# Turning a bias with DVE and ACT instead of TensorE, in the prologue of a fused LayerNorm-MLP kernel

## The chip, the cores and the metric

The kernel runs on one core of one Trainium2 chip. The metric is device time in microseconds, as the median of several executions; lower is better. A profile of one execution lies beside it, and times inside the text are counted from the start of that execution's span.

## The reference

```python
B, S, D, F = 1, 2048, 1024, 3584      # bfloat16 x, w1, b1, w2, b2

def reference(x, w1, b1, w2, b2):
    y = _layernorm(x, axis=-1)        # no scale, no shift, eps 1e-5
    h = _gelu(jnp.einsum("bsd,df->bsf", y, w1) + b1)     # tanh form
    return jnp.einsum("bsf,fd->bsd", h, w2) + b2
```

The bias `b1` has 3584 values. The kernel computes the hidden layer transposed, with the hidden index on the partitions, so `b1` must stand as 28 columns of 128 partitions (`b1_sb`, float32). There ACT takes one column as the per-partition bias of each Gelu.

## The kernel before

Rows of x are handled in 16 tiles of 128 rows, four tiles to a block of 512. The hidden dimension is cut into 28 row blocks of 128 (`FT = 28`), the model dimension into 8 blocks of 128 (`DT = 8`). For each block of x the first product makes `hT_sb` (28 row blocks, 8 matmuls of 128x128x512 each, line 370), ACT applies bias and Gelu out of PSUM (line 396), and the second product goes through all 28 row blocks for each output tile (line 438), after which DVE adds `b2` (line 449) and SP stores. While TensorE works on one block, DVE normalises and transposes the next (lines 254 to 310).

The first block is different, because nothing is there yet. It goes as follows.

- SP issues the loads of x tiles and w1 pieces in a fixed order. ACT's queue issues two loads: `b1`, then the first w1 piece (`w0`). Tile 0 of x is the first load on SP's queue.
- TensorE runs 25 warm-up matmuls on constants (line 460). Then, in the order of the program, it turns `b1` (`pe_b1`, line 521), transposes x tiles 0 and 1 against an identity (line 331), and begins a "wave" of eight row blocks (`pe_wave`, line 386) on the raw, not yet centred tiles 0 to 2, with the transposes of half of tile 2 in between. Tile 3 enters the wave last, normalised.
- ACT copies the transposed tiles out of PSUM (line 343), casts the turned bias into `b1_sb` (`put_b1`, line 525), moves part of tile 2 (`put_moves_2`, line 509), spreads the row of means over the partitions (`put_row_spread`, line 475), moves part of tile 3 (line 516), and only then begins the Gelus.
- DVE takes the statistics of tiles 0 to 3 (lines 254, 264), turns the other half of tile 2 by 32x32 blocks (`turn_2`, line 492), turns means and reciprocal deviations into rows (line 469), normalises tile 3 and turns it (lines 268, 479), centres the raw tiles (line 538), and corrects the raw products in PSUM (`ops_fix`, lines 545 and 548).
- POOL computes the reciprocal deviations (line 261) and moves the remaining blocks of tiles 2 and 3 (lines 505, 484).

Each engine works through its own list strictly in order. The lists are written out by `pe.op`, `act.op`, `dve.op`, `pool.op` and `sp.op`, each with the events that it waits for and the event that it signals; `_emit` turns them into semaphore waits. The list of DVE for the first block is the sequence `seq`. Names of events that the text uses: `b1` (load landed), `b1t` (bias turned), `b1c` (bias in `b1_sb`; every Gelu waits for it), `xq2` (half of tile 2 turned by DVE), `tup2` and `tua2` (moved by POOL and by ACT), `te3`, `tg3`, `tc3` (tile 3 moved), `row_0` and `row_1` (rows spread).

The bias goes through three steps. It is loaded as 28 rows of 128 values into `b1r_sb`. TensorE turns it against a 28x28 corner of the identity into PSUM bank 1 of `ps_1`, and ACT casts the 128x28 result into `b1_sb`. The event of that cast is also recorded as the last reader of the bank, so the wave's second unit waits for it.

Of the kernel before, what the change touches and what calls it, by code (L numbers as in the profile page):

```python
# [7 lines left out]
BF16 = mybir.dt.bfloat16  # L8
F32 = mybir.dt.float32
# [3 lines left out]
P = 128  # L13
# [83 lines left out]
def bass_standalone__mixer_channel_mlp__prompt_kernel(  # L97
# [11 lines left out]
    F = w1.shape[1]  # L109
    NT = ST // P  # L110
    DT = D // P
    FT = F // P
# [2 lines left out]
    DH = D // NCH  # L115
    HC = D // 2
    assert ST % TB == 0 and D % P == 0 and F % P == 0 and D % NCH == 0
    assert HC <= 512 and DT * P * 2 <= 2048 and FT >= 4 and FT <= P
    R = R_WAVE
    assert R == NB1 + NB2 + 1 and R < FT  # L120
    assert NB1 + NB2 + 1 <= 8 and NB2 == 2
# [25 lines left out]
    with ExitStack() as es:  # L147
        sb = lambda name, shape, dt: es.enter_context(nc.sbuf_tensor(name, shape, dt))
# [6 lines left out]
        hT_sb = sb("hT_sb", [P, FT, TB], BF16)  # L155
        o_sb = sb("o_sb", [P, NOB, D], BF16)
        b2_sb = sb("b2_sb", [P, D], BF16)
        b1r_sb = sb("b1r_sb", [FT, P], BF16)
        b1_sb = sb("b1_sb", [P, FT], F32)
        ident = sb("ident", [P, P], BF16)  # L160
        ones = nc.const_aps.tensor(1.0, [P, P], BF16)
        stat_r = sb("stat_r", [P, len(RAW), 4], F32)
# [17 lines left out]
        pe = _Prog("s_pe")  # L180
        act = _Prog("s_act")
# [10 lines left out]
        def dma(dst, src, sig, nbytes, waits=()):  # L192
            dma_q[0].op(lambda e, dst=dst, src=src: e.dma_start(dst, src), waits=waits, sig=sig, sem="d_" + sig, inc=16)
            dma_bytes[0] += nbytes
            est[sig] = DMA_T0 + dma_bytes[0] / DMA_BYTES_PER_US

        def load_x_tile(i):
            dma(x_sb[:, i, :], xf[i * P:(i + 1) * P, :], f"x{i}", P * D * 2)
            x_ev[i] = (f"x{i}", f"x{i}")
# [7 lines left out]
        def load_w1(ci):  # L207
            j0, j1, a, b = w1_chunks[ci]
            dma(w1_sb[:, j0:j1, a:b], w1v[:, j0:j1, a:b], f"w1c{ci}", (j1 - j0) * P * (b - a) * 2)
            w1_issued.add(ci)  # L210
# [5 lines left out]
        def issue(item):  # L216
            if item == "b1":
                dma_q[0] = act
                dma(b1r_sb[:, :], b1.rearrange("(t p) -> t p", p=P), "b1", F * 2)
                dma_q[0] = sp  # L220
            elif item[0] == "x":
                load_x_tile(int(item[1:]))
            elif item[0] == "w" and int(item[1:]) < len(w1_chunks):
                dma_q[0] = act if item == "w0" else sp
                load_w1(int(item[1:]))
                dma_q[0] = sp

        act.op(lambda e: e.preload_act_table(ACT.Gelu_apprx_tanh))
        for item in SP_FIRST_LOADS:
            issue(item)  # L230
# [8 lines left out]
        for b in range(2, NB):  # L239
# [4 lines left out]
                sig="ident")  # L244
# [7 lines left out]
        def op_stats(i, h):  # L252
            pw = D // parts(i)
            return (lambda e, i=i, h=h, pw=pw: e.bn_stats(st_sb[i][:, 6 * h:6 * (h + 1)],  # L254
                                                          x_sb[:, i, h * pw:(h + 1) * pw]),
                    [x_ev[i][h if len(x_ev[i]) == parts(i) else 0]], f"st{i}_{h}", 0.03 + pw * 0.0012)

        def op_aggr(i):
            mv = stat_r[:, i, 0:2] if i in RAW else mv_sb[:, i, :]
            dst = stat_r[:, i, 2:3] if i in RAW else rstd_sb[:, i:i + 1]  # L260
            pool.op(lambda e, i=i, dst=dst, mv=mv: e.tensor_tensor(out=dst, in0=mv[:, 1:2], in1=nhalf[:, i:i + 1],  # L261
                                                                   op=ALU.pow),
                    waits=[f"mv{i}", "nhalf"] + (["tup2"] if i == 1 else []), sig=f"rstd{i}")
            return (lambda e, i=i, mv=mv: e.bn_aggr(mv, st_sb[i][:, :]),  # L264
                    [f"st{i}_{parts(i) - 1}", f"eps{i}"], f"mv{i}", 0.33)
# [9 lines left out]
        def ops_norm(i):  # L275
            cuts = (0, DT)
            y_ev[i] = []
            res = []
            for k, (j0, j1) in enumerate(zip(cuts[:-1], cuts[1:])):
                res.append(op_norm(i, j0 * P, j1 * P, f"y{i}_{k}"))  # L280
                y_ev[i] += [f"y{i}_{k}"] * (j1 - j0)
            return res
# [32 lines left out]
        def dve_put(o):  # L315
# [3 lines left out]
        bank_read = {}  # L319
        bank_of = {"t": ps_t[:, 0, :], "2_0": ps_2b[:, 0, :], "2_1": ps_2b[:, 1, :], "1_1": ps_1b[:, 1, :], "1_2": ps_1b[:, 2, :], "1_3": ps_1b[:, 3, :],  # L320
                   "1_4": ps_1b[:, 4, :]}
# [40 lines left out]
        def unit_bank(bank):  # L362
            return ps_tf if bank[0] == "t" else (ps_1 if bank[0] == "1" else ps_2)[:, bank[1], :]
# [30 lines left out]
        def act_gelu(r, t0, t1, bank, wait_ev, sig):  # L394
            n0, n1 = t0 * P, t1 * P
            act.op(lambda e, r=r, n0=n0, n1=n1, bank=bank: e.activation(  # L396
                out=hT_sb[:, r, n0:n1], in_=unit_bank(bank)[:, n0:n1], func=ACT.Gelu_apprx_tanh,
                bias=b1_sb[:, r:r + 1], scale=1.0),
                waits=[wait_ev, "b1c"], sig=sig)
            bank_gelu[bank] = sig  # L400

# [76 lines left out]
        def moves_3():  # L478
            res = [(lambda e: e.transpose(out=xq_sb[:, :], in_=x_sb[:, 3, :]), [y_ev[3][-1], "tua2", "tup2"], "xq", 1.07)]
            for tq, q in POOL_MOVES + DVE_MOVES:  # L480
                src = xq_sb[32 * tq:32 * (tq + 1), :].rearrange("p (j q s) -> p j q s", j=DT, q=4)[:, :, q, :].bitcast(I32)
                dst = yT_sb[32 * q:32 * (q + 1), ybuf(0), :, ycol(3) + 32 * tq:ycol(3) + 32 * (tq + 1)].bitcast(I32)
                if (tq, q) in POOL_MOVES:
                    pool.op(lambda e, src=src, dst=dst: e.tensor_copy(out=dst, in_=src), waits=["xq"],
                            sig=("tg3" if (tq, q) == POOL_MOVES[-1] else None))
                if (tq, q) in DVE_MOVES:
                    res.append((lambda e, src=src, dst=dst: e.tensor_copy(out=dst, in_=src), ["xq"],
                                ("tc3" if len(res) == len(DVE_MOVES) else None), 0.2))
            return res

        def turn_2():
            return [(lambda e: e.transpose(out=xq_sb[:, 0:(DT - N_TURN) * P], in_=x_sb[:, 2, N_TURN * P:]),
                     [x_ev[2][0]], "xq2", 0.64)]

        def put_moves_2(eng):
            todo = POOL_TURNS
            if eng is act:
                todo = [m for m in ((tq, q) for tq in range(4) for q in range(4)) if m not in POOL_TURNS]
            for n, (tq, q) in enumerate(todo):
                src = xq_sb[32 * tq:32 * (tq + 1), 0:(DT - N_TURN) * P]  # L500
                src = src.rearrange("p (j q s) -> p j q s", j=DT - N_TURN, q=4)[:, :, q, :].bitcast(I32)
                dst = yT_sb[32 * q:32 * (q + 1), 0, N_TURN:DT, ycol(2) + 32 * tq:ycol(2) + 32 * (tq + 1)].bitcast(I32)
                sig = "tup2" if eng is pool else "tua2"
                if eng is pool:
                    pool.op(lambda e, src=src, dst=dst: e.tensor_copy(out=dst, in_=src),
                            waits=["xq2"] + {0: ["rstd0"], 4: ["tup2_0"]}.get(n, []),
                            sig={3: "tup2_0", 7: sig}.get(n))
                else:
                    act.op(lambda e, src=src, dst=dst: e.copy(out=dst, in_=src), waits=["xq2"], sig=(sig if n + 1 == len(todo) else None))
# [7 lines left out]
                       sig=("te3" if (tq, q) == todo[-1] else None))  # L517
            yT_ev[3] = ["te3"] * DT

        def pe_b1():  # L520
            pe.op(lambda e: e.transpose(out=bank_of["1_1"][:, 0:FT], in_=b1r_sb[:, :], identity=ident[0:FT, 0:FT]),  # L521
                  waits=["ident", "b1"], sig="b1t")

        def put_b1():
            act.op(lambda e: e.copy(out=b1_sb[:, :], in_=bank_of["1_1"][:, 0:FT]), waits=["b1t"], sig="b1c")
            bank_read["1_1"] = "b1c"

        row_b = lambda k: row_r[:, :, :].rearrange("p (t k) s -> p t k s", k=2)[:, :, k, :]
        raw_cols = lambda bank, c0: unit_bank(bank)[:, c0:c0 + len(RAW) * P].rearrange("p (t s) -> p t s", t=len(RAW))
# [21 lines left out]
        st = {0: [op_stats(0, 0), op_stats(0, 1), op_aggr(0)]}  # L551
        put_moves_2(pool)
        st.update({i: [op_stats(i, 0), op_stats(i, 1), op_aggr(i)] for i in range(1, TPB)})
        nm = {3: ops_norm(3)}
        turn_m, turn_r = ops_row_turn(0), ops_row_turn(1)
        ctr = ops_centre()
        seq = st[0] + st[1][:1] + turn_2() + st[1][1:] + st[2] + turn_m[:2] + st[3] + turn_m[2:] + nm[3] + moves_3() + turn_r + ctr[:2]
        for o in seq:
            dve_put(o)

        pe_b1()
        put_b1()
        T_BANKS = (("t", "2_0"), ("2_1", "1_4"), ("t", "2_0"))
        for t, j in [(0, j) for j in range(N_AHEAD)] + [(1, j) for j in range(GROUPS[1])] + [
                (0, j) for j in range(N_AHEAD, DT)] + [(1, j) for j in range(GROUPS[1], DT)]:
# [19 lines left out]
        for k in range(2):  # L585
            put_copy(2, G2, T_BANKS[2], k)
        put_moves_2(act)
        for j in range(N_TURN, DT):
            yT_ev[2][j] = "tua2"
        put_row_spread(0, 1, 4)  # L590
# [136 lines left out]
```

## Time and profile before

| | |
|---|---|
| median of 3 runs | 396.33 us (396.06 to 396.37) |
| profiled execution, its own time | 396.51 us |
| its span | 395.3 us |
| TensorE matmul busy | 390.9 us (99% of the span), 1916 instructions |
| DVE busy | 162.7 us (41%) |
| ACT busy | 87.1 us (22%) |
| POOL busy | 14.0 us (4%) |
| line 438 (second product) | 193.3 us of TensorE |
| line 370 (first product, blocks after the wave) | 152.4 and 31.9 us of TensorE |
| line 386 (the wave) | 14.4 and 3.2 us of TensorE |

A line of the time line gives the start of a group of instructions, its length, the engine, the source line, the operation, what it writes and reads, how many there are, and in brackets the idle time of the engine ahead of it and what ended that. "PEld" is the weight load of TensorE, which overlaps its matmuls ("PE"); "SPq" and "ACTq" are DMA issues on those engines' queues. Matmuls are pipelined, so that the length of one in the list is longer than the distance to the next.

### The profile page before, as it was taken

Reading aid. Unit: us, or ns where it says so; the run is one execution under the profiler, and the core shown is the slowest. Engines: PE = TensorE matmul, PEld = TensorE weight load, DVE = VectorE, ACT = ScalarE, POOL = GpSimd, SP = SyncE. Lnnn points to the kernel's source line nnn. Section 1 sums busy time; section 2 is a strip of 40 time slices with the busy share of each in tenths; the row PEclk is TensorE's granted clock in tenths of the full one; section 3 lists DMA queues with packets and bytes.
Section 4 is the critical chain, followed back from the end, with each engine's and each line's share of the span. In section 5 each row is a group of like instructions: output and inputs, shape, how many; then the busy total and the mean of one; then the engine's idle time right before and its main releaser. Section 6 shows DMA issues by size and latency. Waiting matters only on the chain.

```text
span 395.3 us, 4562 instructions
## 1 busy us (share of the span) xinstructions
PE 390.9 (99%) x1916; PEld 185.8 (47%) x1950; DVE 162.7 (41%) x339; ACT 87.1 (22%) x145; POOL 14.0 (4%) x69
## 2 busy tenths in 40 slices
PE   9999999999999999999999999999999999999998
PEld 8744444444444444444444444444444444444444
DVE  6998889998999306987100000001100000001011
ACT  5655420000134332000023443000003334400000
POOL 5201000011001100000000000000000000000000
PEclk9999999999999999999999999999999999999999
DMA  7999930000000000000000000000000000000000
GB/s 273 375 385 387 387 139 27 15 27 14 28 0 0 2 0 0 28 27 15 27 13 2 0 0 2 13 13 28 25 15 15 0 2 0 0 15 27 13 28 27
DMA packets 16078, 23.63 MB, mean 60 GB/s; under 512 B 1082, under 2 KB 8250, under 8 KB 16058
## 3 DMA queue, kind: packets, MB, share of 16 engines
q1 hardware_dynamic: 15872, 23.20, 16.5%
q8 instruction: 15, 0.25, 0.3%
q10 hardware_dynamic: 186, 0.14, 0.1%
q14 instruction: 5, 0.04, 0.0%
HBM read 19.14 MB, written 4.19 MB: 59 GB/s over the span
## 4 chain that ended last, share of the span: by engine, by line
PE 99%; issue 0%; DVE 0%
PE ps L438 49%; PE ps L370 38%; PE ps_t L370 7%; PE ps L386 3%; PE ps L460 1%; PE ps_t L386 0%; PE ps L331 0%; PE ps_t L331 0%; DVE o_sb L449 0%; PE ps L521 0%
## 5 line engine op out<-in xcount | busy, mean ns | idle before, releaser
L438 PE MATMUL ps<-w_sb,hT_sb 128*128 128x512 bf16 (+2 forms) x909 | 193.3, 373 | 0.8
L370 PE MATMUL ps<-yT_sb,w_sb 128*128 128x512 bf16 x678 | 152.4, 379 | 0.9
L438 PEld LDWEIGHTS ps<-w_sb,hT_sb 128*128 128x128 bf16 x924 | 88.6, 98 | 105.2
L396 ACT ACTIVATE hT_sb<-ps,b_sb 128x512 bf16<-128x512 f32 x94 | 64.0, 688 | 234.9 <-PE ps L370 217.2
L370 PEld LDWEIGHTS ps<-yT_sb,w_sb 128*128 128x128 bf16 x696 | 68.1, 98 | 81.9
L449 DVE TENSOR_TENSOR o_sb<-ps,b_sb 128x512 bf16<-128x512 f32 (+2 forms) x33 | 22.3, 676 | 198.7 <-PE ps L438 198.5
L310 DVE STREAM_TRANSPOSE yT_sb<-x_sb 32x256 bf16<-32x256 bf16 x192 | 83.7, 436 | 21.9 <-PE ps_t L370 18.8
L370 PE MATMUL ps_t<-yT_sb,w_sb 128*128 128x512 bf16 x135 | 31.9, 379 | 0.1
L254 DVE BATCH_NORM_STATS2 st_sb<-x_sb 128x6 f32<-128x512 bf16 x32 | 21.1, 671 | 3.5 <-DMA x_sb<-in_x_dram 3.4
L370 PEld LDWEIGHTS ps_t<-yT_sb,w_sb 128*128 128x128 bf16 x136 | 13.3, 98 | 16.1
L396 ACT ACTIVATE hT_sb<-ps_t,b_sb 128x512 bf16<-128x512 f32 x18 | 12.4, 687 | 17.1 <-PE ps_t L370 14.6
L386 PE MATMUL ps<-yT_sb,w_sb 128*128 128x128 bf16 (+3 forms) x132 | 14.4, 262 | 0.0
L386 PEld LDWEIGHTS ps<-yT_sb,w_sb 128*128 128x128 bf16 x132 | 10.0, 101 | 2.8
L261 POOL TENSOR_TENSOR rstd_sb<-mv_sb,nhalf 128x1 f32<-128x1 f32 x13 | 7.1, 548 | 111.7 <-DVE mv_sb L264 111.7
L412 DVE TENSOR_TENSOR ps<-ps,row_r 128x384 f32<-128x384 f32 x17 | 9.2, 563 | 3.1 <-PE ps L370 2.8
L268 DVE TENSOR_SCALAR x_sb<-x_sb,mv_sb,rstd_sb 128x1024 bf16<-128x1024 bf16 x13 | 7.0, 541 | 2.0 <-POOL rstd_sb L261 1.3
L545 DVE SCALAR_TENSOR_TENSOR ps<-row_r,ncs,ps 128x384 f32<-128x384 f32 x7 | 4.2, 614 | 0.5 <-PE ps L386 0.5
L548 DVE TENSOR_TENSOR ps<-ps,row_r 128x384 f32<-128x384 f32 x7 | 3.9, 563 | 0.2
L538 DVE TENSOR_TENSOR yT_sb<-yT_sb,row_r 128x768 bf16<-128x768 bf16 x4 | 3.6, 952 | 0.0
L460 PE MATMUL ps<-const-bfloat16-1.0 128*128 128x128 bf16 x25 | 2.8, 312 | 0.8 <-PEq L712 0.8
L475 ACT COPY row_r<-row_r 32x384 f32<-32x384 f32 x6 | 3.1, 509 | 2.2 <-DVE row_r L469 2.1
L386 PE MATMUL ps_t<-yT_sb,w_sb 128*128 128x386 bf16 (+1 forms) x16 | 3.2, 273 | 0.0
(37 smaller groups left out, 36.9 us busy)
## 6 DMA issues: line engine op xcount, KB each, us to landing
w_sb<-in_w_dram SPq DMA_DIRECT2D x4, 1792.0 KB, 18.3
w_sb<-in_w_dram SPq DMA_DIRECT2D x2, 2048.0 KB, 15.8
out_dram<-o_sb SPq DMA_DIRECT2D x31, 128.0 KB, 1.7
x_sb<-in_x_dram SPq DMA_DIRECT2D x3, 1024.0 KB, 14.5
w_sb<-in_w_dram SPq DMA_DIRECT2D x7, 256.0 KB, 5.5
x_sb<-in_x_dram SPq DMA_DIRECT2D x4, 256.0 KB, 3.3
w_sb<-in_w_dram SPq DMA_DIRECT2D x1, 1024.0 KB, 9.3
b_sb<-in_b_dram SPq DMA_DIRECT2D x1, 256.0 KB, 14.4
```

What stands on the lines that cost most here:

```text
L254: return (lambda e, i=i, h=h, pw=pw: e.bn_stats(st_sb[i][:, 6 * h:6 * (h + 1)], x_sb[:, i, h * pw:(h + 1) * pw]), [x_ev[i][h if len(x_ev[i ...
L261: pool.op(lambda e, i=i, dst=dst, mv=mv: e.tensor_tensor(out=dst, in0=mv[:, 1:2], in1=nhalf[:, i:i + 1], op=ALU.pow), waits=[f"mv{i}", "nh ...
L268: return (lambda e, i=i, c0=c0, c1=c1: e.tensor_scalar(out=x_sb[:, i, c0:c1], in0=x_sb[:, i, c0:c1], scalar1=mv_sb[:, i, 0:1], scalar2=rst ...
L310: res.append((lambda e, src=src, dst=dst: e.transpose(out=dst, in_=src), waits, (f"tr{i}" if lastop else None), 0.47))
L370: pe.op(lambda e, b=b, r=r, dt=dt, bank=bank: e.matmul(unit_bank(bank)[:, 0:TB], lhsT=w1_sb[:, dt, r * P:(r + 1) * P], rhs=yT_sb[:, ybuf(b ...
L386: pe.op(lambda e: e.matmul(unit_bank(bank)[:, n0:n1], lhsT=w1_sb[:, dt, r * P:(r + 1) * P], rhs=yT_sb[:, 0 if tiles[0] in RAW else ybuf(0) ...
L396: act.op(lambda e, r=r, n0=n0, n1=n1, bank=bank: e.activation(out=hT_sb[:, r, n0:n1], in_=unit_bank(bank)[:, n0:n1], func=ACT.Gelu_apprx_tanh,
L412: crit.append((est[sig], (lambda e, reg=reg: e.tensor_tensor(out=reg, in0=reg, in1=row_b(1), op=ALU.mult), [sig, "row_1"], ready, 0.57), 0))
L438: pe.op(lambda e, sl=sl, ft=ft, c0=c0, c1=c1, bank=bank: e.matmul(ps_2[:, bank, 0:c1 - c0], lhsT=hT_sb[:, ft, sl * P:(sl + 1) * P], rhs=w2 ...
L449: crit.append((est[sig], (lambda e, ob=ob, c0=c0, c1=c1, bank=bank: e.tensor_tensor(out=o_sb[:, ob, c0:c1], in0=ps_2[:, bank, 0:c1 - c0], ...
L460: pe.op(lambda e: e.matmul(ps_1[:, 0, 0:P], lhsT=ones, rhs=ones, start=True, stop=True))
L545: return [(lambda e: e.scalar_tensor_tensor(out=reg, in0=row_b(0), scalar=ncs[:, c:c + 1], in1=reg, op0=ALU.mult, op1=ALU.add), [f"m1_0_{r ...
```

## The change

The load of `b1` fills 32 rows instead of 28: rows 0 to 15, and rows 12 to 27 as a second group of 16, so that rows 12 to 15 stand there twice. DVE turns the 32x128 array as four 32x32 blocks in one instruction, ahead of everything else on its list. ACT then copies each of the four blocks, with a cast to float32, to its own 32 partitions of `b1_sb`; these four copies stand behind ACT's moves of tile 2. The Gelu's column index is mapped (`b1_col`): columns 0 to 15 are unchanged, column r from 16 on is column r + 4. The TensorE transpose and its PSUM bank are gone from this path, and with them the wait of the wave's second unit.

```diff
-    assert HC <= 512 and DT * P * 2 <= 2048 and FT >= 4 and FT <= P
+    assert 16 <= FT <= 32 and HC <= 512 and DT * P * 2 <= 2048 and FT >= 4 and FT <= P
...
-        b1r_sb = sb("b1r_sb", [FT, P], BF16)
-        b1_sb = sb("b1_sb", [P, FT], F32)
+        b1r_sb = sb("b1r_sb", [32, P], BF16)
+        b1t_sb = sb("b1t_sb", [32, P], BF16)
+        b1_sb = sb("b1_sb", [P, 32], F32)
...
-                dma(b1r_sb[:, :], b1.rearrange("(t p) -> t p", p=P), "b1", F * 2)
+                rows = bass.AP(b1.tensor, b1.offset, [[(FT - 16) * P, 2], [P, 16], [1, P]])
+                dma(b1r_sb[:, :], rows, "b1", 32 * P * 2)
...
-                bias=b1_sb[:, r:r + 1], scale=1.0),
+                bias=b1_sb[:, b1_col(r):b1_col(r) + 1], scale=1.0),
...
-        def pe_b1():
-            pe.op(lambda e: e.transpose(out=bank_of["1_1"][:, 0:FT], in_=b1r_sb[:, :], identity=ident[0:FT, 0:FT]),
-                  waits=["ident", "b1"], sig="b1t")
+        b1_col = lambda r: r if r < 16 else r + 32 - FT
+        turn_b1 = (lambda e: e.transpose(out=b1t_sb[:, :], in_=b1r_sb[:, :]), ["b1"], "b1t", 0.25)

         def put_b1():
-            act.op(lambda e: e.copy(out=b1_sb[:, :], in_=bank_of["1_1"][:, 0:FT]), waits=["b1t"], sig="b1c")
-            bank_read["1_1"] = "b1c"
+            for q in range(4):
+                act.op(lambda e, q=q: e.copy(out=b1_sb[32 * q:32 * (q + 1), :], in_=b1t_sb[:, 32 * q:32 * (q + 1)]),
+                       waits=["b1t"], sig=("b1c" if q == 3 else None))
...
-        seq = st[0] + st[1][:1] + turn_2() + ...
+        seq = [turn_b1] + st[0] + st[1][:1] + turn_2() + ...
...
-        pe_b1()
-        put_b1()
...
         put_moves_2(act)
+        put_b1()
```

More of the change, by code (lines that the diff above doesn't have):

```diff
@@ L556, in bass_standalone__mixer_channel_mlp__prompt_kernel @@
         ctr = ops_centre()
-        seq = st[0] + st[1][:1] + turn_2() + st[1][1:] + st[2] + turn_m[:2] + st[3] + turn_m[2:] + nm[3] + moves_3() + turn_r + ctr[:2]
+        seq = [turn_b1] + st[0] + st[1][:1] + turn_2() + st[1][1:] + st[2] + turn_m[:2] + st[3] + turn_m[2:] + nm[3] + moves_3() + turn_r + ctr[:2]
         for o in seq:
             dve_put(o)
-        pe_b1()
-        put_b1()
         T_BANKS = (("t", "2_0"), ("2_1", "1_4"), ("t", "2_0"))
```

## The prediction

> **What bounds the kernel now.** I read the page first, then the time line of the first 22 us, because the change touches only that stretch. Chances and verdicts below use 0.2% (0.8 us) as what a measurement of this kernel can tell from no change.
>
> ```profile
> PE 390.9 (99%) x1916; PEld 185.8 (47%) x1950; DVE 162.7 (41%) x339; ACT 87.1 (22%) x145; POOL 14.0 (4%) x69
> ...
> PE 99%; issue 0%; DVE 0%
> ```
>
> TensorE is busy for 390.9 of 395.3 us, and the chain that ended last runs 99% through it. Outside the start and the last store there is almost nothing to win, and anything that makes TensorE late is passed on to the end in full. So the question is when TensorE gets its operands in the first 22 us. The time line there:
>
> ```profile
> 0.81 0.63 ACTq L193 DMA_DIRECT2D b1r_sb<-in_b_dram  x1
> 0.83 2.83 PE L460 MATMUL ps<-const-bfloat16-1.0 128*128 128x128 bf16 x25 [0.83 <-PEq L712]
> 1.47 0.37 ACTq L193 DMA_DIRECT2D w_sb<-in_w_dram  x1
> 3.43 1.29 DVE L254 BATCH_NORM_STATS2 st_sb<-x_sb 128x6 f32<-128x512 bf16 x2 [3.43 <-DMA x_sb<-in_x_dram]
> 3.58 0.10 PEld L521 LDWEIGHTS ps<-ident,b1r_sb 28*128 28x128 bf16 x1 [0.20 <-issue]
> 3.58 0.20 PE L521 MATMUL ps<-ident,b1r_sb 28*128 28x28 bf16 x1
> 3.72 0.39 PE L331 MATMUL ps_t<-ident,x_sb 128*128 128x128 bf16 x2
> 3.82 0.18 ACT L525 CAST b_sb<-ps 128x28 f32<-128x28 bf16 x1 [1.76 <-PE ps L521]
> 5.45 0.69 DVE L492 STREAM_TRANSPOSE xq_sb<-x_sb 128x512 bf16<-128x512 bf16 x1
> 6.20 2.15 POOL L505 COPY yT_sb<-xq_sb 32x64 int32<-32x64 int32 x8 [0.58 <-DVE xq_sb L492]
> 7.03 2.01 ACT L509 COPY yT_sb<-xq_sb 32x64 int32<-32x64 int32 x8
> 11.12 1.55 ACT L475 COPY row_r<-row_r 32x384 f32<-32x384 f32 x3 [2.07 <-DVE row_r L469]
> 17.35 1.15 DVE L545 SCALAR_TENSOR_TENSOR ps<-row_r,ncs,ps 128x384 f32<-128x384 f32 x2 [0.54 <-PE ps L386]
> ```
>
> Columns: start, length, engine, line, operation. Four things are to be seen. The bias's small matmul (L521) comes between the warm-up (L460) and the transposes of x (L331), with 0.20 us of idle ahead of its weight load. DVE's first work waits for x until 3.43. ACT has 2.07 us free ahead of 11.12. DVE has 0.54 us free ahead of 17.35; between 3.43 and there it works almost without a break, so a late start of DVE moves all of it.
>
> The semaphore records add the landings: b1 is complete at 3.15, x tile 0 at 3.41, x tile 1 at 4.25, the first w1 piece (behind b1 on ACT's queue) at 4.58.
>
> **The change, part by part.**
>
> *TensorE loses the bias matmul.* The last warm-up matmul starts at 3.34; at its spacing of 0.107 us the next could start at 3.44. The first transpose of x starts at 3.72. So 0.27 us lie free, and x tile 0 (3.41) allows about 3.45. But the seventh transpose in program order is of x tile 1: its weight load waits for that landing and starts at 4.29 (landing 4.25 plus 0.04), its matmul at 4.33, in step with the six before. With those six 0.27 us earlier, the seventh still cannot start before about 4.29. Of 0.27 us, 0.04 are kept and 0.23 become a wait for x tile 1: -0.04 us, and -0.27 at most were x tile 1 earlier too.
>
> *The PSUM bank and the ACT copy ahead.* Bank 1_1 no longer waits for the copy of b1, and ACT's 0.18 us at 3.82 goes. ACT's next copy waits for TensorE anyway. Nothing either way; with that cover gone, 0.18 us.
>
> *ACT gets four copies of 32x32 behind its moves of tile 2.* The moves end at 9.05. A 32x128 copy takes 0.30 us (L516), a 32x64 one 0.24 (L509), the 128x28 cast 0.18: 0.22 each, 0.9 together, to 9.95. The next ACT work begins at 11.12, when DVE's row turn is there. Nothing; without that cover 0.9 us on the mean row, which the first fix (18.40) needs, with little of it reaching TensorE. The first Gelu, which needs the bias, starts at 19.00.
>
> *DVE gets a block transpose as its first instruction, waiting for b1.* 128x512 takes 0.69 us (L492), 128x1024 1.25 (L479), 32x256 0.44 (L310): 0.15 fixed and 1.1 ns per column, so 32x128 is 0.29 us. Behind it in DVE's order stands everything: statistics of tile 0, the turn of tile 2, the mean row, the normalisation of tile 3, the fixes. With b1 landing at L, DVE starts on x at L + 0.03 + 0.29, against 3.43 now: it is late by D = L - 3.11. If L stays at 3.15, D is 0.04.
>
> What D costs TensorE comes from four covers. (a) POOL's moves end at 8.35 and follow DVE's turn (6.13) one for one; TensorE's weight load that needs them starts at 9.61: cover 1.2 us. (b) ACT's moves start at 7.03, though the turn is done at 6.14; they end at 9.05, the same load needs them: 0.9 of D passes unseen, then 0.56 more. (c) The moves of tile 3 end at 15.05 and 15.17, needed at 16.54: 1.3 us. (d) DVE's 0.54 us idle ahead of 17.35, then the last centring, which ends at 21.15 and whose matmul (row 8, seventh of eight) is due at 21.57: 0.54 + 0.39, so 0.93 us. The first to give is (d): TensorE is late by D - 0.93, that is, from L = 4.04 on, and by 0.8 us from L = 4.85 on.
>
> *So when does b1 land?* Now 28 rows of 256 B; its records show one early step at 1.53, before any packet, and 14 completions from 2.92 to 3.15, so 14 of the 16 DMA engines took two rows each (128-row loads show 16 completions). Two groups of 16 can be split as 16 engines with two rows each, or as two engines with sixteen rows each. In the first case L stays near 3.15. In the second, 14 more rows go through one engine. A row's packet takes 15 to 18 ns; the two rows of one engine started 0.092 us apart, one 2048 B packet of x (84 ns) between. So 14 rows add 0.25 us at least and 1.29 us at most: L is 3.40 to 4.44, D 0.29 to 1.33, the cost 0 to 0.40 us. I take L = 3.8 (D = 0.7, cost 0): rows took turns with x tile 0 singly, but the eight w1 packets of each engine went through in one run 42 ns apart, without x between, so sixteen rows will do some of both.
>
> The Trainium skill, "DMA: Bandwidth & Descriptors", section "Why a DMA increments its semaphore by 16 and not by 1", speaks against this load: a queue-issued transfer uses the largest number of engines, up to 16, that divides the slowest dimension of both sides. By that rule the trace's 14 engines for 28 rows agree, and an outer dimension of two gives two engines; the sum by it is the second case.
>
> *The other loads.* Two engines with 14 more rows finish x tile 1 up to 0.25 us later (14 x 18 ns); its completions spread from 3.87 to 4.25, so a typical engine hides most of it. Bounds: -0.05 (the 14 relieved engines) to +0.25; I take +0.10. The first w1 piece sits behind b1 on the same queue: 4.58 plus 0.25 to 1.29 is 4.83 to 5.87 on those two engines, needed at 5.29, so 0 to 0.58; I take 0, as for L.
>
> **Sum.** The profiled execution took 396.51 us, span 395.28 with 1.23 around it; it is 0.18 above the median 396.33. -0.04 + 0.10 = +0.06 gives 396.57, and on the median 396.4. The bounds are -0.32 (-0.27 - 0.05) and +0.98 (0.40 + 0.58 if fully added, though the waits partly overlap).
>
> **Rivals.**
>
> *N: sixteen engines keep the load as it is.* L = 3.15, D = 0.04, TensorE -0.04: 396.3. For it: every other load here uses at least 14 engines. Against: a split into equal shares, as 28 = 14 x 2, does not come out of an outer dimension of two.
>
> *S, slower: b1 on two engines takes its turns against whole shares of SP's loads.* An engine's share of x tile 1 is eight packets, 0.66 us, and the w1 packets waited for all of it. If five rows pass with tile 0 by 2.85 and the other eleven come four to a share, three shares of 0.66 and 0.37 from the last packet to the landing give L = 5.2, D = 2.1, TensorE late by 1.2: 397.6. Two to a share: six shares, L = 7.2, about +3.1: 399.5. One to a share: L above 10, and the w1 piece behind it would hold TensorE from 5.29 to 11: +6. It decides from L = 4.85. For it: the run of eight in the w1 packets. Against: b1's own rows went singly between packets of tile 0.
>
> *G, faster: the early stretch runs at the full matmul rate sooner.* Up to 6.58 matmuls of 128 columns start 0.107 us apart, then 0.056. If closing the gap at 3.44 to 3.72 let the faster rate begin at 4.25, 1.17 us would be saved, cut to 0.87 by the w1 piece that lands at 9.24 and is used at 10.11: 395.5. Against: the same length of gap reappears ahead of 4.29, waiting for x tile 1. The Trainium skill, "TensorE: Matmul & The Clock Gate", Part 1, puts this change of rate down to an activity window of about 3.4 us that runs freely; by that rule a shift of a 0.27 us gap moves nothing.
>
> **How the numbers follow.** Forecast (two engines, hidden or nearly) 0.57, of which 0.04 end past +0.8; N 0.12; S 0.22; G 0.09, of which 0.01 stay within 0.8. So faster 0.08, same 0.66 (0.53 + 0.12 + 0.01), slower 0.26. The likeliest gives 396.4, its own range 396.0 to 397.3. The range for 8 in 10 takes in the four-to-a-share case of S and most of G's way down: 395.7 to 398.2.
>
> **What would show it.** Right: no L521 row; the first L331 matmul near 3.45 and a gap of about 0.2 us ahead of its seventh; b1 with two completions with data, landing 3.4 to 4.4; DVE's transpose in front, its statistics late by the same; four ACT casts near 9 to 10 us; no idle of TensorE at 9.6, 16.5 or 21.4 above 0.4 us. Wrong: a landing of b1 past 4.85, a wait at 5.3 for the first w1 piece or at 9.6 for POOL's moves, or the 0.107 us spacing ending more than a microsecond away from 6.58.

## The result and the profile after

The changed kernel takes 396.98 us as the median of 19 runs (396.49 to 399.33), the kernel before 396.10 in the same comparison (19 runs, 395.66 to 396.63). The ratio is 1.0037, 95% interval 1.0023 to 1.0051: slower, by more than the 0.2% that the prediction took as the limit. The median lies 0.88 us higher; the ratio says more than that, because 6 of the 19 runs lie at 398.9 to 399.3. The median of the other 13 is 396.94.

The profiled execution of the changed kernel is one of the quickest, 396.49 us with a span of 395.3, so its span shows no loss against before's 395.3. The loss has to be read inside. Page, then the time line of the first 22 us (start, length, engine, line, operation):

```profile
PE 392.2 (99%) x1949; PEld 185.1 (47%) x1949; DVE 162.8 (41%) x340; ACT 87.8 (22%) x148; POOL 14.0 (4%) x69
...
PE 98%; DMA 1%; DVE 0%; POOL 0%; issue 0%; ACT 0%
```

```profile
0.83 1.24 ACTq L194 DMA_DIRECT2D b1r_sb<-in_b_dram  x1
2.10 0.36 ACTq L194 DMA_DIRECT2D w_sb<-in_w_dram  x1
...
3.53 0.30 DVE L523 STREAM_TRANSPOSE b1t_sb<-b1r_sb 32x128 bf16<-32x128 bf16 x1 [3.53 <-DMA b1r_sb<-in_b_dram]
...
3.66 0.37 PE L333 MATMUL ps_t<-ident,x_sb 128*128 128x128 bf16 x2
...
3.77 1.23 DVE L256 BATCH_NORM_STATS2 st_sb<-x_sb 128x6 f32<-128x512 bf16 x2
...
5.96 0.61 PE L388 MATMUL ps<-yT_sb,w_sb 128*128 128x130 bf16 x8 [0.43 <-POOL stat_r L263]
...
6.47 2.15 POOL L507 COPY yT_sb<-xq_sb 32x64 int32<-32x64 int32 x8 [0.58 <-DVE xq_sb L494]
...
7.04 2.01 ACT L511 COPY yT_sb<-xq_sb 32x64 int32<-32x64 int32 x8
...
9.07 0.90 ACT L527 CAST b_sb<-b1t_sb 32x32 f32<-32x32 bf16 x4
...
11.39 1.55 ACT L477 COPY row_r<-row_r 32x384 f32<-32x384 f32 x3 [1.42 <-DVE row_r L471]
...
17.33 1.15 DVE L547 SCALAR_TENSOR_TENSOR ps<-row_r,ncs,ps 128x384 f32<-128x384 f32 x2 [0.26 <-PE ps L388]
```

Three things are new. The issue of b1 holds ACT's queue for 1.24 us instead of 0.63, so the issue behind it, the first w1 piece, begins at 2.10 instead of 1.47. TensorE begins its wave (L388) at 5.96 instead of 5.40, after an idle time. And DVE is 0.34 us late at its first statistics, 0.28 at POOL's moves, 0.27 at the row spread, and not at all at 17.33: its covers took it. Before's row of the wave, for comparison:

```profile
5.40 1.07 PE L386 MATMUL ps<-yT_sb,w_sb 128*128 128x130 bf16 x8
```

The profile puts the idle time ahead of 5.96 down to POOL's line 263. That line is only the last to have signalled; the event of POOL that the wave waits for is the memset of the ones, done by 1.3. The semaphore records show the w1 piece complete at 5.82, and TensorE's wait for it passed at 5.85. In a second profile of the same kernel, where nothing else signals in between, the waits of TensorE (engine and line, released by, total, times, longest) name it:

```profile
PE ps L388 <- DMA w_sb<-in_w_dram: 1.9, 1, 1.9
```

Why do the spans agree at 395.3, with the wave 0.56 us later? Before ran its first matmuls of the wave at the early spacing, 0.107 us for 128 columns, until 6.58, which cost it 0.58 (span minus the start of the wave is 389.89 there, 389.31 in after's profile); in this profile of the changed kernel the spacing was 0.056 from the wave's first matmul on. Also, the profiled execution of before (396.51) lies near the top of its kernel's 19 runs, and that of the changed kernel at the bottom of its own.

### The profile page after: what moved, and what is told of

Its sections match the earlier page's. It is cut to its first block, busy times and chain, and to the rows that moved or that the text cites. A ratio compares the mean times of both kernels' runs of the same rounds, so it can differ in the third digit from the quotient of the medians.

```text
span 395.3 us, 4598 instructions
## 1 busy us (share of the span) xinstructions
PE 392.2 (99%) x1949; PEld 185.1 (47%) x1949; DVE 162.8 (41%) x340; ACT 87.8 (22%) x148; POOL 14.0 (4%) x69
## 4 chain that ended last, share of the span: by engine, by line
PE 98%; DMA 1%; DVE 0%; POOL 0%; issue 0%; ACT 0%
PE ps L440 49%; PE ps L372 38%; PE ps_t L372 7%; PE ps L388 3%; DMA b1r_sb<-in_b_dram 1%; PE ps_t L388 0%; DVE st_sb L256 0%; POOL stat_r L263 0%; DVE stat_r L266 0%; DVE o_sb L451 0%; PE ps L333 0%; PE ps_t L333 0%; DVE b1t_sb L523 0%; ACT L230 0%
## 5 line engine op out<-in xcount | busy, mean ns | idle before, releaser
L388 PE MATMUL ps<-yT_sb,w_sb 128*128 128x128 bf16 (+3 forms) x132 | 14.0, 257 | 0.4 <-POOL stat_r L263 0.4
L388 PEld LDWEIGHTS ps<-yT_sb,w_sb 128*128 128x128 bf16 x132 | 9.6, 98 | 3.5 <-POOL stat_r L263 0.7
L388 PE MATMUL ps_t<-yT_sb,w_sb 128*128 128x386 bf16 (+1 forms) x16 | 3.2, 273 | 0.0
```

The lines of the kernel that those rows point to most:

```text
L388: pe.op(lambda e: e.matmul(unit_bank(bank)[:, n0:n1], lhsT=w1_sb[:, dt, r * P:(r + 1) * P], rhs=yT_sb[:, 0 if tiles[0] in RAW else ybuf(0) ...
```

## The experiments

Below, "wave" is the start of the first wave matmul, "landed" the last semaphore record of the first w1 piece; both, and the issues, from each kernel's own profile. Each ratio is against the kernel before on the same chip (medians 396.10 to 396.31 in these comparisons). In the comparison that holds "before, sixteen", "sixteen, late", "w1 on SP" and "six fills", two of the 35 runs of the kernel before lie at 398.31 and 398.43, which widens these four intervals.

| kernel | b1 issue, us | w1 piece issued | landed | wave | span | median | ratio, 95% |
|---|---|---|---|---|---|---|---|
| before | 0.63 | 1.47 | 4.58 | 5.40 | 395.28 | | |
| before again | 0.63 | 1.47 | 5.32 | 5.46 | 395.25 | 396.29 | 1.0003 (0.9994 to 1.0012) |
| after | 1.24 | 2.10 | 5.82 | 5.96 | 395.27 | 396.98 | 1.0037 (1.0023 to 1.0051) |
| after again | 1.24 | 2.10 | 7.09 | 7.22 | 396.53 | 397.62 | 1.0039 (1.0025 to 1.0053) |
| load only | 1.23 | 2.10 | 6.84 | 6.97 | 396.28 | 397.81 | 1.0049 (1.0032 to 1.0066) |
| turn late | 1.24 | 2.10 | 6.65 | 6.79 | 396.10 | 397.34 | 1.0035 (1.0021 to 1.0048) |
| w1 first | 1.20 | 0.81 | 4.07 | 5.72 | 396.70 | 397.97 | 1.0043 (1.0030 to 1.0056) |
| sixteen engines | 0.68 | 1.55 | 6.21 | 6.34 | 397.50 | 396.74 | 1.0022 (1.0010 to 1.0034) |
| before, sixteen | 0.70 | 1.56 | 6.39 | 6.53 | 396.23 | 397.05 | 1.0018 (1.0004 to 1.0032) |
| sixteen, late | 0.68 | 1.55 | 5.77 | 5.91 | 395.22 | 396.75 | 1.0010 (0.9995 to 1.0025) |
| w1 on SP | 1.22 | 1.69 | 5.47 | 5.61 | 395.38 | 396.90 | 1.0016 (1.0005 to 1.0027) |
| old load | 0.64 | 1.48 | 4.62 | 4.89 | 394.81 | 396.28 | 1.0002 (0.9993 to 1.0011) |
| six fills | 1.24 | 2.10 | 6.77 | 6.91 | 396.22 | 397.44 | 1.0032 (1.0018 to 1.0045) |
| fourteen fills | 1.23 | 2.09 | 6.11 | 6.24 | 395.55 | 397.11 | 1.0029 (1.0020 to 1.0039) |

One regularity carries most of what follows. In seven of these profiles (after, after again, load only, turn late, sixteen late, and both with fills), span minus wave is 389.30 to 389.32. From the wave on, TensorE in these seven never waits again in the prologue, and every 0.1 us by which the w1 piece lands later is 0.1 us of span.

The landings also show what the piece lost. In both profiles of before and in "old load" it is issued ahead of x tile 2 (SP, at 1.69) and lands 0.68 to 0.98 us ahead of it. In the six profiles with the load in two groups in front of it on ACT's queue it is issued behind x tile 2 (2.09 to 2.10 against 1.69 to 1.70) and lands 0.17 to 0.20 us behind it. x tile 2 itself landed anywhere from 5.26 to 6.92 (6.21 in "before again"), so a very late w1 piece is in part a late x tile 2; with the piece back in time, x tile 2 is what TensorE waits for next, as in "before again", "old load" and "w1 on SP".

Two theories are set against each other in the expectations: W, that the loss comes from the late w1 piece, and D, that it comes from DVE's late start. (D also stands for that delay itself, as in the prediction.)

**Load only.** The kernel before with the new load and nothing else; TensorE still turns the bias.

```diff
-                dma(b1r_sb[:, :], b1.rearrange("(t p) -> t p", p=P), "b1", F * 2)
+                rows = bass.AP(b1.tensor, b1.offset, [[(FT - 16) * P, 2], [P, 16], [1, P]])
+                dma(b1r_sb[:, :], rows, "b1", 32 * P * 2)
...
-            pe.op(lambda e: e.transpose(out=bank_of["1_1"][:, 0:FT], in_=b1r_sb[:, :], identity=ident[0:FT, 0:FT]),
+            pe.op(lambda e: e.transpose(out=bank_of["1_1"][:, 0:32], in_=b1r_sb[:, :], identity=ident[0:32, 0:32]),
```

> The kernel before with one part of the change: the load of b1 as two groups of 16 rows (and a bias array of 32 columns to fit). TensorE still turns it, now 32 rows, and ACT casts once. Theory W (the first w1 piece comes late, because its issue stands on ACT's queue behind the issue of b1, 1.24 us long instead of 0.63): w1 piece issued near 2.1, landed near 5.8, a wait of TensorE of 0.5 to 0.7 us ahead of the first L386 matmul, the bias matmul late too (b1 at 3.5); time like after's, 396.7 to 397.2, with a few runs near 399. Theory D (DVE starts 0.34 us late and the delay goes through its list to TensorE): DVE is as early as before, so time like before, 395.9 to 396.4.

Measured 397.81 us (10 runs, 396.79 to 399.65), no quicker than the whole change. TensorE's waits:

```profile
PE ps L387 <- DMA w_sb<-in_w_dram: 1.7, 1, 1.7
```

The load alone brings the loss; DVE has no part in this kernel's bias. Theory D falls here.

**Turn late.** After, with DVE's turn moved out of the front.

```diff
-        seq = [turn_b1] + st[0] + ...
+        seq = st[0] + ... + ctr[:2] + [turn_b1]
...
-        put_b1()
...
         put_row_spread(1, 3, 4)
+        put_b1()
```

> After with DVE's transpose of the bias moved from the front of its list to the end of the sequence of the first block (behind the first two centrings), and ACT's four copies moved behind the last spread of the reciprocal row. The load is after's. W: the w1 piece is as late as in after (5.8), the wait at 5.2 stays, time 396.6 to 397.2 with a few near 399. D: DVE starts at 3.4 to 3.5, time back to 395.9 to 396.4.

397.34 us (10 runs, 396.93 to 399.60). DVE starts on x at 3.43, exactly as in before, and nothing is won; TensorE waits for the same piece:

```profile
PE ps L388 <- DMA w_sb<-in_w_dram: 1.5, 1, 1.5
```

**W1 first.** After, with the two loads on ACT's queue exchanged.

```diff
-SP_FIRST_LOADS = ("b1", "x0", "x1", "w0", "x2", ...
+SP_FIRST_LOADS = ("w0", "b1", "x0", "x1", "x2", ...
```

> After with the two loads on ACT's queue exchanged: the first w1 piece, then b1. DVE's transpose still stands in front. W: the w1 piece is issued near 0.85 and lands by 4.5, no wait at 5.2; b1 is issued near 1.2 for 1.2 us and lands at 3.9 to 4.3, DVE is late by 0.8 to 1.2 us, which its covers take up to 0.9; time 395.8 to 396.5. D: DVE is two to three times as late as in after, so slower than after, 397.5 or more.

397.97 us (5 runs, 396.88 to 398.58): the time expected by D, by another price. The w1 piece lands at 4.07 and the wait for it is gone. But x tile 0, which shares the engines with it, lands at 3.90 instead of 3.41 to 3.53, and b1 only at 5.49. DVE's time line, then TensorE's waits:

```profile
5.52 0.30 DVE L523 STREAM_TRANSPOSE b1t_sb<-b1r_sb 32x128 bf16<-32x128 bf16 x1 [5.52 <-DMA b1r_sb<-in_b_dram]
5.75 1.23 DVE L256 BATCH_NORM_STATS2 st_sb<-x_sb 128x6 f32<-128x512 bf16 x2
```

```profile
PE ps L388 <- POOL yT_sb L507: 0.6, 1, 0.6
PE ps_t L333 <- DMA x_sb<-in_x_dram: 0.4, 1, 0.4
```

DVE is 2.32 us late, two to three times the expected 0.8 to 1.2, and now it does reach TensorE: through POOL's moves, at 9.87 to 10.77. The delay of DVE is harmless at 0.34 and costs at 2.32. This run shows why the bias must not be turned ahead of the statistics unless its load is early, and W is borne out only in that the wait at 5.2 went.

**Sixteen engines.** After, with the two outer dimensions of the load exchanged, and the column index to match.

```diff
-                rows = bass.AP(b1.tensor, b1.offset, [[(FT - 16) * P, 2], [P, 16], [1, P]])
+                rows = bass.AP(b1.tensor, b1.offset, [[P, 16], [(FT - 16) * P, 2], [1, P]])
...
-        b1_col = lambda r: r if r < 16 else r + 32 - FT
+        b1_col = lambda r: 2 * r if r < 16 else 2 * (r - FT + 16) + 1
```

> After with the order of the two dimensions of the b1 load exchanged: 16 pairs of rows instead of two groups of 16, so that the two copies lie interleaved; the column index is mapped to match. Everything else as after. W: if the long issue comes from the outer dimension of two, the issue takes 0.63 us or less, 16 completions with data, the w1 piece lands near 4.6 as before, no wait at 5.2, time 395.8 to 396.3 and no runs near 399. If the issue stays at 1.2 us, the time stays near 397. D: DVE's transpose still stands in front, b1 lands near 3.15, D falls to 0.05, so D expects before's time as well; this run does not part W from D, but tells whether the split of the load is the cause of either.

The issue is 0.68 us, a little over the 0.63 expected, and there are 16 completions, as expected. The time is 396.74 us (12 runs; ten at 396.43 to 397.20, two at 398.73 and 398.75): a smaller loss than after's, though the intervals of the two ratios overlap, and not before's time, so that W's 395.8 to 396.3 was missed. The w1 piece is issued at 1.55, 0.08 us later than in before, but its issue takes 0.59 us instead of 0.37, and it lands at 6.21 and not near 4.6. The packets show where: in before an engine's eight w1 packets start 0.042 us apart, ahead of those of x tile 2; here, on the last engines, they start 0.122 us apart, in turns with x tile 2's packets (84 ns each).

This profile fell on one of the two runs at 398.7, and shows what such a run is. TensorE's time line:

```profile
3.88 1.70 PE L333 MATMUL ps<-ident,x_sb 128*128 128x128 bf16 x14
6.34 1.02 PE L388 MATMUL ps<-yT_sb,w_sb 128*128 128x130 bf16 x8 [0.76 <-DMA w_sb<-in_w_dram]
7.15 0.42 PE L333 MATMUL ps_t<-ident,x_sb 128*128 128x128 bf16 x2
```

Line 333's two matmuls at 7.15 stand 0.107 us apart. That was the spacing ahead of the wait, too, and apart from the wave's first two matmuls (0.059 apart, as the first two behind other waits are) it stays at 0.107 to 0.111 until about 10.2; then it is 0.056 for good. In all other profiles it is 0.056 by 6.8. Span minus wave is 391.16 here, 1.84 us above the seven.

**Before, sixteen.** The kernel before with this load; TensorE turns the 32 rows. (Edit: the load line and column index of "sixteen engines" in the kernel of "load only".)

> The kernel before with the load of b1 as 16 pairs of rows; TensorE turns the 32 rows, ACT casts once: the load of the run with sixteen engines without DVE's part. W: the issue is 0.63 to 0.7 us, the w1 piece lands within 0.3 us of before's on most engines; time 396.1 to 396.5. If the time is as with sixteen engines and DVE (396.7), what is left over there comes from the load; if it is before's 396.3, it comes from DVE's late start (D) or from the missing bias matmul.

397.05 us (11 runs, 396.59 to 398.98), with the w1 piece at 6.39: W's 396.1 to 396.5 was missed, too. The remainder comes from the load here as well, not from DVE.

**Sixteen, late.** The edits of "sixteen engines" and "turn late" together.

> The load as 16 pairs of rows, DVE's transpose at the end of the sequence of the first block, ACT's four copies behind the last spread of the reciprocal row. D: if DVE's start at 4.03 (0.6 late) made the 0.4 us that were left with sixteen engines, the time is 396.1 to 396.4. W: what is left comes from the landing of the w1 piece, so 396.5 to 396.9, as with sixteen engines.

396.75 us (12 runs, 396.33 to 398.48), ratio 1.0010 with an interval that holds 1. The median agrees with W's expectation; the ratio does not part the two.

**W1 on SP.** After, with the first w1 piece issued by SP between x tiles 1 and 2.

```diff
-                dma_q[0] = act if item == "w0" else sp
+                dma_q[0] = sp
```

> After with one thing changed: the first w1 piece is issued on SP's queue (between x tiles 1 and 2), so that b1 is alone on ACT's queue and its long issue delays nothing. The load of b1 as two groups, DVE's transpose in front. W: the w1 piece lands by 5.0, no wait at 5.2, time 396.0 to 396.5, no runs near 399. x tile 2 is issued some 0.4 us later, which DVE's turn of it may feel. D: DVE still starts 0.3 to 0.4 late, so the time stays near 397.

396.90 us (11 runs, 396.58 to 397.85). The wave starts at 5.61, and there is no run near 399. But x tile 2 and the second w1 piece, now behind it, hold TensorE again (matmuls 0.23 and 0.26 us apart, start to start, at 6.0 and 6.4): part of the wait was moved. W's 396.0 to 396.5 was missed.

**Old load.** After, but the load of before on ACT's queue; the four rows to make 32 come by a second small load behind the ninth w1 piece; the turn late, as above.

```diff
-                rows = bass.AP(b1.tensor, b1.offset, [[(FT - 16) * P, 2], [P, 16], [1, P]])
-                dma(b1r_sb[:, :], rows, "b1", 32 * P * 2)
+                dma(b1r_sb[0:FT, :], b1.rearrange("(t p) -> t p", p=P), "b1", F * 2)
...
+            elif item == "pad":
+                dma(b1r_sb[FT:32, :], b1.rearrange("(t p) -> t p", p=P)[FT - 4:FT, :], "pad", 4 * P * 2)
```

> After with the old load of b1: 28 rows in one transfer on ACT's queue, as in before. The four rows that the block transpose needs beyond them come from a second small load on SP's queue behind the ninth w1 piece. DVE's transpose stands at the end of the sequence of the first block, ACT's four copies behind the last spread of the reciprocal row; column index unchanged. So TensorE has no part in the bias and the start of the loads is before's. W: all of the loss was the load; issue 0.63 us, w1 piece by 4.7, no wait at 5.2, time 395.9 to 396.3, ratio 0.999 to 1.001. If the time stays at 396.7 or above, the loss comes from taking the bias matmul away or from ACT's later copies.

396.28 us (11 runs, 396.04 to 396.59), ratio 1.0002, interval 0.9993 to 1.0011: the loss is gone, with TensorE out of the bias as in after. Its time line:

```profile
0.81 0.64 ACTq L194 DMA_DIRECT2D b1r_sb<-in_b_dram  x1
1.48 0.36 ACTq L194 DMA_DIRECT2D w_sb<-in_w_dram  x1
...
4.89 0.61 PE L389 MATMUL ps<-yT_sb,w_sb 128*128 128x130 bf16 x8
5.65 0.28 PE L334 MATMUL ps_t<-ident,x_sb 128*128 128x128 bf16 x2
...
16.92 0.29 DVE L524 STREAM_TRANSPOSE b1t_sb<-b1r_sb 32x128 bf16<-32x128 bf16 x1
...
17.28 0.90 ACT L528 CAST b_sb<-b1t_sb 32x32 f32<-32x32 bf16 x4
18.75 1.26 ACT L399 ACTIVATE hT_sb<-ps,b_sb 128x512 bf16<-128x512 f32 x2 [0.57 <-DVE ps L551]
```

The issue times of before are back, the turn lies in DVE's gap ahead of the first fix, and the four casts end 0.57 us before the first Gelu. What TensorE waits for now is x tile 2: it lands at 5.60, and its transposes begin at 5.65, 0.31 us behind their turn. Nor is anything gained against before: the free place on TensorE is worth nothing that these runs resolve.

**Before again, after again.**

> The kernel before, unchanged, as one of the compared kernels: it shows how far two sets of runs of the same kernel lie apart (0.999 to 1.001 if the comparison is sound) and gives a second profile of before for the landings. W needs the first w1 piece to land ahead of 5.3 here too; if it lands later without a loss of time, W falls.

> The changed kernel, unchanged, on the same chip: 396.8 to 397.2 for most runs, a third near 399. W: the w1 piece issued near 2.1 again, landed near 5.8 or later, TensorE waiting for it.

Two sets of runs of before differ by 0.03%. In its second profile the w1 piece lands at 5.32, and TensorE, here at the spacing of 0.056 from 4.1 on, waits for it as well, until 5.46, and then for x tile 2. TensorE's waits here:

```profile
PE ps L386 <- DMA w_sb<-in_w_dram: 0.5, 1, 0.5
PE ps_t L331 <- DMA x_sb<-in_x_dram: 0.2, 1, 0.2
```

So before stands at the edge: the piece was needed at 5.29 in its first profile, where the spacing was 0.107 until 6.58, and by 4.8 in this one. With the load in two groups it lands 0.5 to 1.8 us past 5.29 in every profile that has it behind that load on ACT's queue. The changed kernel had 5 runs here, 397.24 to 398.48, and none near 399.

**Six and fourteen fills.** After, with matmuls on constants between the transposes and the wave.

```diff
             pe_T_one(t, GROUPS, T_BANKS[t], j)
+        warm(14)
```

> After with six more matmuls on constants put between the transposes of x tiles 0 and 1 and the first matmul of the wave (0.64 us at the early spacing of 0.107 us), so that TensorE works while it waits for the first w1 piece. Their results are overwritten. Theory R (the runs near 399, 6 of 19 in after, are those in which the idle time at 5.2 lies so that the full matmul rate comes one step later): no runs near 399, the rest unchanged near 396.9 or up to 0.2 later, median 396.7 to 397.1. If the runs near 399 have another cause (a landing that is later still, say), about a third of the runs stay there.

> After with fourteen more matmuls on constants ahead of the wave (1.5 us at the spacing of 0.107 us, 0.8 at 0.056), so that TensorE is not idle until the w1 piece is there. R: no runs near 399, but up to 0.9 us more in the others: median 397.0 to 397.9, highest under 398.4. If runs near 399 remain as often as with the changed kernel beside it, R is not the cause.

With six: 397.44 us, two of 12 runs at 398.94 and 399.25; in its profile 0.81 us of idle time stayed, so it did not test R. With fourteen: 397.11 us, nine runs, the highest 397.91. That agrees with R, but in its profile, too, a gap stayed (0.65 us from start to start ahead of the wave), and the unfilled kernel beside it had no run near 399 either, in five.

The late step to the full rate that R names is shown in one trace (sixteen engines). Counting does not settle that the wait brings it on, and the kernel before, with the old load, has two of 35 runs near 398.4. The granted TensorE clock on record beside each run speaks for a stretch at less than full rate in the longest runs: it is 0.996 in 10 of the 12 runs from 398.9 up and 1.0 in every other run that has it. An estimate from this is 0.4% of 398 us, 1.6 us, most of the 2 us or so by which these runs are longer. A clock of 1.0 does not rule such a stretch out, for the run traced at 398.73 has 1.0 beside a spacing of 0.107 until 10.2.

## Why the prediction was right or wrong

The forecast was no change, at 396.4 us with a range of 395.7 to 398.2. The median 396.98 lies in the range, but the ratio says slower: the likeliest case did not come, and the slower side, given 0.26, did. That the range held the result is owed to its width: 0.22 of the 0.26 were for rival S, a late b1, which did not happen, and what came is a sign that the prediction itself had listed as one of being wrong, a wait at 5.3 for the first w1 piece.

**The step that failed is "The other loads".** It put the w1 piece at 4.83 to 5.87, allowed 0 to 0.58 us for the wait, and took 0. Measured were 5.82 and 7.09, waits of 0.64 and 2.07 (idle of the matmul slots: start to start, 0.745 and 2.123, less the spacing of 0.107 and 0.056). That 5.82 lies inside the bounds is luck: they were worked out from b1's extra rows, and b1 came 0.36 us later, the piece 1.24. The time of need, 5.29, was read from one profile as well; in the second one of before the transposes were done by 4.8. Its mechanism was also short: it counted b1's rows ahead of the piece in the queue and not the issue instruction. The issue's row stood in the prediction's time line (0.63 us on ACT's queue, and the w1 piece's right behind it), and the change doubled it. The rest is the piece's lost place: 3.10 us from issue to landing in before's profile, 3.72 and 4.99 in after's, now behind x tile 2. No run parts the two: with sixteen engines both issues are done by 2.14 instead of 1.84, and the piece still lands at 6.21.

**When b1 lands.** Right in kind. The records of b1's semaphore show one step at 2.16 and two completions, 3.49 and 3.51: two engines with sixteen rows each. The Trainium skill's rule ("DMA: Bandwidth & Descriptors", "Why a DMA increments its semaphore by 16 and not by 1"), the largest number up to 16 that divides both sides' slowest dimension, agrees with that, with 16 completions after the exchange, and with 14 for 28 rows. The sixteen rows of an engine started 0.014 us apart, not 0.092, so L is 3.51, near the lower end (3.40) and not the 3.8 taken, and D is 0.34 instead of 0.7. Rival N (sixteen engines) and rival S (turns against whole shares) did not happen.

**DVE, ACT and the covers.** The turn took 0.30 us against 0.29 worked out, the four casts 0.90 against 0.9. D cost nothing, as said; DVE's 0.54 us of idle time shrank to 0.26. "W1 first" tried the covers with D = 2.32: POOL's moves (cover 1.2) held TensorE, 0.3 late already by x tile 0, for 0.79, and 2.32 - 1.2 - 0.3 is 0.8; the last centring, cover (d), then held a weight load at 22.84. Span and median there are about 1.4 and 1.7 above before's; D - 0.93 is 1.39.

**TensorE without the bias matmul.** The transposes begin at 3.66, not 3.45, because x tile 0 landed at 3.53; in "turn late" (landing 3.41) they begin at 3.54 and the seventh stands at 4.31, held by x tile 1 (4.26), as argued. The -0.04 drowns. The +0.10 for x tile 1 did not come: it landed at 4.21 (4.29 in the second profile), against 4.25 in before.

**Rival G** did not come as a gain; its mirror did, unforeseen, in one profile: with a wait of 0.96 us ahead of the wave the full rate began at about 10.2 instead of 6.6. That the wait put it off is not shown.

## What to carry to other kernels

When a load's shape is changed, cost its issue on the queue as well as its landing, and name the next load on that queue with the time by which it is needed: here 7 to 8 KB of bias moved a 128 KB weight piece. Look at a start-up stage for the operand that lands last before the bound engine, and read its slack from more than one profile. A wait in the profile that names an engine long done is to be checked against the landings.

## What the runs showed of the hardware

- The issue of a small load from ACT's queue: 28 rows on 14 engines 0.63 us, 32 rows as 16 pairs on 16 engines 0.68 to 0.70, two groups of 16 rows on two engines 1.20 to 1.24. The 128 rows of the w1 piece take 0.35 to 0.39, but 0.59 to 0.60 when they follow the 16 pairs; and SP's third issue takes 0.62 instead of 0.42 beside the long one.
- Packets of two queues take turns one by one on an engine (b1's rows in before 0.092 us apart; w1 packets 0.122 apart beside x tile 2), but in other places the rows of one queue go through in a run (b1's in after 0.014, w1 packets in before 0.042 apart). What decides it is not shown.
- The matmul spacing for 128 columns goes from 0.107 to 0.056 us at a time that differs from run to run: at 4.1 and at 6.58 in the two profiles of before, by 6.8 in all but one, and at about 10.2 in the profile at 398.7, behind a wait of 0.96 us. Other waits ahead of the wave, of 0.5 to 2.1 us, were followed by 0.056 throughout. The Trainium skill, "TensorE: Matmul & The Clock Gate", Part 1, has an activity window of about 3.4 us that runs freely; a step at such different times agrees with that, while the window's length is shown by no run here.
